# Eight more halved steps in three of 25 blocks of a fused FFT and FFN kernel

## The chip, the cores and the metric

The kernel runs on one core of one Trainium2 chip. The metric is the device time of one execution in microseconds. A core has five engines, each with an instruction queue of its own that is worked off in order: PE (TensorE: matmuls; PEld is its weight load), DVE (VectorE), ACT (ScalarE), POOL (GpSimd, which here mainly issues transfers) and SP (SyncE, which issues the stores). They wait for each other through semaphores.

## The reference

```python
def _attn_ref(x) -> np.ndarray:          # x: 8 x 3008 x 256
    X = np.fft.fft(x, axis=1)
    X = np.fft.fft(X, axis=2)
    return X.real.astype(np.float32)

def _moe_ref(x, w_in, w_out):            # 24064 x 256, 256 x 2048, 2048 x 256
    h = np.maximum(x @ w_in, 0.0)
    return (h * h @ w_out).astype(np.float32)
```

The real part of a two-dimensional Fourier transform of each of 8 batches gives 24064 rows of 256. Each row goes through a matrix to 2048 values, a Relu, a square, and a matrix back to 256.

## The kernel before

The transform is done by matrix products with tables of sines and cosines, after the input has been folded along its symmetries. It is real, so row k and row S - k of the result have most of their work in common. If P is the part from the cosine sums (tile `zc`) times the folded first matrix (`gh[:, 0]`) and Q the part from the sine sums (`zs`, `gh[:, 1]`), then one row's value ahead of the Relu is P + Q, and its mirror row's is P - Q, but for a correction of one row of the sine part (weights `wv`, spread sine row `eb`).

**Blocks and steps.** The columns of `zc` and `zs` (one for each pair of rows) are cut into 25 blocks, `w` = 0 to 24, of 240, 512, 376, 376, 512, 448 and then mostly 512 columns. The "third", "fourth" and "seventh" block are `w` = 2, 3 and 6, and the "fifth" and "eighth" `w` = 4 and 7. A block has 8 steps, 0 to 7; a step makes 256 of the 2048 values for the block's columns. They go, squared, into the tile `h2`, first all plain columns, then all mirrored ones. Blocks of less than 384 columns ahead of a wider one make the wider one take its steps in twos (`ng` = 2: the second and the fifth block); the blocks that the change touches take them one by one.

**A plain step** (`pq`, `turn`, `square`): PE makes P + Q in four matmuls over the block's width (lines 801 and 802), ACT applies the Relu (L811), the result is squared by DVE (L816) or, for the steps in the second list of the plan, by ACT (L814). PE then adds -2Q in place by two matmuls with a third matrix (L807), which makes the mirrored values; ACT applies the Relu (L811) and DVE squares (L816).

**A halved step** (`half_q`, `half_p`, `row_sum`, `halves`): PE makes Q alone in two matmuls (L826), ACT copies -2Q to `sn` (L834), PE adds P in place in two matmuls (L840), ACT copies P + Q to `hd` (L842). The rest is done by DVE, for one or two steps together as the plan groups them: the corrections `eb` x `wv` ("rows", L850, one for each 128 values), added to `sn` (L854), `hd` + `sn` into the mirrored half (L864), the Relu over both halves (L865) and the square into `h2` (L866). A halved step thus has four matmuls in place of six, and more work for DVE. L850 and L854 of a group are queued when its last step's Q is made; L864, L865 and L866 of a group are queued one step later, between the rows of the next group if that step is halved too.

**Between the two halves of a step** run, in this order, the step's list `at[s]` (folding of later batches, making of tables), a share of the second matrix product of the block before (`ffn2`, L680: 16 matmuls in most steps, 8 in some where that block is narrower; L695 copies out and SP stores), and a share of the sums `z` that make the next block's `zc` and `zs` (matmuls L536; ACT copies the plain part, L541 and L545; DVE makes the mirrored part, L552, when the last matmul of a sum is queued). The next block's first matmul (L801) reads `zc`.

**Work of single blocks.** In the third block a second pair of tables is made: arguments on DVE (L254 to L274), sine and cosine on ACT (L277, L280), then weights on DVE in the last step (L285). The z sums of the fourth block read them. The fold of batches on DVE there is L447 and L458, after which POOL copies edges into `spn` (L464 to L466), which some z matmuls read. `row_weights` (L632, L633) makes `wv`, with 16 small matmuls into one of the accumulators of the second product. POOL issues the spreading of a sine row for the next block (`row_spread`, L642, `eb`) near the end of a block, after step 5 or 6 in most, if the next block has halved steps.

**Buffers.** `sn` rotates over two tiles, `hd` over two buffers that it shares with the argument tile of the tables, `eb` over two that it shares with a table input, first-product accumulators (`ph`) over two, second-product accumulators over two, and `h1` over five.

**The plan.** For each block it lists the groups of halved steps and the plain steps that ACT squares. Before, the first three blocks have no halved step; the fourth has steps 1, 2 and 4; the fifth 2 and 3; the seventh 1, 2, 4 and 5, with ACT squaring in steps 0, 3 and 6.

```python
    PLAN = {
        6: (((1, 2), (3, 4), (5, 6)), (0, 7)),
        5: (((1, 2), (3, 4), (5,)), (0, 6, 7)),
        4: (((1, 2), (4, 5)), (0, 3, 6)),
        3: (((1, 2), (4,)), (0, 5, 6)),
        2: (((2, 3),), ()),
    }
```

Each engine's instructions run in the order in which the kernel's code queues them (`tc.manual_schedule()`); waits are put in from the tiles that are read and written.

Of the kernel before, what the change touches and what calls it, by code (L numbers as in the profile page):

```python
# [28 lines left out]
def kernel(  # L29
# [36 lines left out]
    }  # L66

    RQ = (1, 3, 5, 0, 2, 4)
# [14 lines left out]
    while g < TOT:  # L83
        n = min(FIRST[len(wins)] if len(wins) < len(FIRST) else WN, TOT - g)
# [4 lines left out]
    def win_of(col):  # L89
        return max(w for w in range(NW) if wins[w][0] <= col) if col < TOT else NW  # L90
# [491 lines left out]
    def run(*jobs):  # L582
        for j in jobs:
            j()
# [132 lines left out]
    def fold_jobs(i):  # L717
        f = folds[i] = fold_steps(i)
        return [f["d_even"], f["n_cos"], f["d_odd"], f["n_sin"], f["odds"], f["nyq"], f["even"], f["back"]]
# [11 lines left out]

    def plan(w):

        if w < 3:
            return (), ()
        if w < 5:
            return PLAN[3 if w == 3 else 2]
        first, late, main = w in first_at, w in late_at, w in fold_at
        n = 4 if main or late else 5 if first or w + 1 == NW or not need[w + 1] else 6
        return PLAN[n - (first and late)]  # L740

    def halved(w):

        return plan(w)[0]
# [4 lines left out]
    for w in range(NW):  # L749
# [5 lines left out]
        at = [[] for _ in range(NST)]  # L755
        post = [[] for _ in range(NST)]
        if w == 0:
            at[2] = [f0s["even"], f0s["back"]]
            at[0] = [lambda: run(*z0(0, 2)), lambda: run(*z0(1, 2))]
        elif w == 1:  # L760
            fj = fold_jobs(1)
            at = [fj[0:1], fj[1:3], fj[3:4], fj[4:5], [], [], [], []]
            post[5] = fj[5:6]
            lo, hi = 6, 7
        elif w == 2:
            te = table_steps()
            at = [[folds[1]["even"], lambda: te["freq"](), lambda: te["args"](0)], [lambda: te["turns"](0)], [lambda: te["mods"](0)],
                  [lambda: te["absm"](0)], [lambda: te["sins"](0)], [lambda: te["coss"](0)], [], [lambda: te["weigh"]()]]
            for st in range(4):
                at[st + 3] = at[st + 3] + f0s["late"][st : st + 1]  # L770
            at[7].append(folds[1]["back"])
        elif w in fold_at:
            fj = jobs_of.pop(fold_at[w])
            at = [fj[2:3], fj[3:4], fj[4:5], [], [], [], fj[6:7], fj[7:8]]
            post[6] = fj[5:6]
        elif w == win_of(col_of[1, 1]) - 1:
            for st in range(4):
                at[st] = folds[1]["late"][st : st + 1]
            lo = 4
# [6 lines left out]
            at[0] = at[0] + fj[0:1]  # L786
            at[1] = at[1] + fj[1:2]
        if w == 2:
            at[2].append(row_weights)
        zj, zl = [], []  # L790
        for u in need[w + 1]:
            zu = z_steps(u)
# [24 lines left out]

        two = {s: g for g in halved(w) for s in g}
        by_act = plan(w)[1]
        sns, hds = {}, {}  # L820

# [173 lines left out]
```

## Time and profile before

| what | value |
| --- | --- |
| median of 3 runs | 600.67 us (600.64 to 600.76) |
| the profiled execution | 600.49 us |
| its span, first to last instruction | 598.7 us |
| granted TensorE clock | full throughout |
| matmuls, weight loads | 4376 each |
| instructions of DVE, ACT, POOL | 747, 661, 152 |
| mean DMA rate over the span | 84 GB/s |
| PE's longest waits, by what ended them | DVE 3.8 (start), ACT sn L834 2.5 (nine), DVE 1.5 (start), DVE 1.2 (first block), DVE h L866 1.1 (two) |

The profile is of one execution. In its groups and timelines a row has a start and a duration in us (or a mean in ns), engine, line, operation, the tiles written and read, and a count; in square brackets stands the idle time ahead of it with what ended it. A row with "x4" is four instructions, its duration from the first start to the last end. A matmul's end is modelled: the next one is issued before it. On DVE and ACT too, an instruction that does not read the result of the one ahead starts a little before that one's shown end.

### The profile page before, as it was taken

How to read it: one execution, taken by the hardware profiler on the slowest of the kernel's cores; microseconds unless marked ns; L12 is line 12 of the kernel's file. 1: busy time of each engine (PE TensorE's matmuls, PEld its weight loads, DVE VectorE, ACT ScalarE, POOL GpSimd, SP SyncE). 2: the span in 40 equal slices, each digit the busy share in tenths (PEclk: the TensorE clock that was granted, in tenths of full speed). 3: DMA queues.
4: the chain of work that ended last, by engine and by line, in shares of the span. 5: the costliest groups of instructions: out<-in, count | busy, mean ns of one | idle time of the engine just before them, and what ended most of it. 6: DMA issues, size and time to landing. Idle time of an engine off the chain costs nothing.

```text
span 598.7 us, 11343 instructions
## 1 busy us (share of the span) xinstructions
PE 579.3 (97%) x4376; PEld 420.6 (70%) x4376; DVE 512.9 (86%) x747; ACT 514.0 (86%) x661; POOL 96.7 (16%) x152
## 2 busy tenths in 40 slices
PE   5899999999999999999999999999999999999996
PEld 2557776776777777777677776777777776776786
DVE  7897578886999987989889899898998799889980
ACT  7687788888999889989889898989989888888882
POOL 6350301202102023030112200412000120000000
PEclk9999999999999999999999999999999999999999
DMA  8945342472444635834355424555133361434122
GB/s 148 204 109 137 49 73 54 54 156 87 64 47 83 135 103 78 124 108 65 44 114 104 107 41 58 105 123 91 47 35 68 70 99 42 52 54 44 61 58 68
DMA packets 37581, 50.31 MB, mean 84 GB/s; under 512 B 4567, under 2 KB 30711, under 8 KB 37527
## 3 DMA queue, kind: packets, MB, share of 16 engines
q0 software_dynamic: 10400, 24.94, 32.0%
q1 hardware_dynamic: 26899, 24.44, 13.6%
q8 instruction: 34, 0.56, 0.4%
q10 hardware_dynamic: 228, 0.21, 0.1%
q14 instruction: 20, 0.16, 0.1%
HBM read 33.63 MB, written 27.84 MB: 103 GB/s over the span
## 4 chain that ended last, share of the span: by engine, by line
PE 67%; DVE 12%; ACT 12%; issue 7%; DMA 1%; POOL 0%; ACTq 0%; DVEq 0%; SPq 0%; POOLq 0%
PE po L680 40%; PE ph L840 5%; PE ph L807 5%; PE ph L801 5%; PE ph L802 5%; PE ph L826 5%; ACT h L811 3%; PE pz L536 3%; ACT sn L834 3%; ACT osb L695 2%; DVE h L866 2%; ACT hd L842 2%; DVE hd L865 2%; DVE hd L864 2%; DVE sn L854 1%
## 5 line engine op out<-in xcount | busy, mean ns | idle before, releaser
L680 PE MATMUL po<-wout,h 128*128 128x256 f16 (+1 forms) x3024 | 362.0, 273 | 1.1 <-DVE h L866 1.1
L680 PEld LDWEIGHTS <-h 128*128 128x128 f16 (+1 forms) x3024 | 296.5, 98 | 72.8 <-DVE h L866 1.7
L811 ACT ACTIVATE h<-ph 128x1024 f16<-128x1024 f32 (+3 forms) x196 | 185.6, 981 | 11.6 <-PE ph L807 8.6
L842 ACT ACTIVATE hd<-ph 128x1024 f16<-128x1024 f32 (+3 forms) x94 | 94.0, 1001 | 14.7 <-PE ph L840 13.3
L866 DVE TENSOR_TENSOR h<-hd 128x4096 f16<-128x4096 f16 (+6 forms) x51 | 105.3, 2065 | 1.4
L816 DVE TENSOR_TENSOR h<-h 128x1024 f16<-128x1024 f16 (+3 forms) x135 | 85.4, 656 | 24.7 <-ACT h L811 21.8
L834 ACT ACTIVATE sn<-ph 128x1024 f16<-128x1024 f32 (+3 forms) x94 | 93.6, 997 | 0.7 <-PE ph L826 0.7
L854 DVE TENSOR_TENSOR sn<-sn,hd 128x2048 f16<-128x2048 f16 (+6 forms) x51 | 56.7, 1113 | 22.6 <-ACT sn L834 18.0
L695 ACT ACTIVATE osb<-po 128x512 f32<-128x512 f32 (+3 forms) x95 | 54.6, 578 | 24.6 <-PE po L680 23.8
L801 PE MATMUL ph<-zc,gh 128*128 128x512 f16 (+3 forms) x196 | 72.1, 368 | 0.5 <-ACT h L897 0.3
L802 PE MATMUL ph<-zs,gh 128*128 128x512 f16 (+3 forms) x196 | 72.1, 368 | 0.0
L864 DVE TENSOR_TENSOR hd<-hd,sn 128x2048 f16<-128x2048 f16 (+6 forms) x51 | 56.6, 1110 | 14.0 <-ACT hd L842 12.1
L814 ACT ACTIVATE h<-h 128x1024 f16<-128x1024 f16 (+3 forms) x61 | 62.7, 1028 | 1.9
L865 DVE TENSOR_SCALAR hd<-hd 128x4096 f16<-128x4096 f16 (+6 forms) x51 | 56.8, 1113 | 1.5
L840 PE MATMUL ph<-zc,gh 128*128 128x512 f16 (+3 forms) x188 | 54.6, 372 | 3.5 <-ACT sn L834 2.5
L807 PE MATMUL ph<-zs,gh 128*128 128x512 f16 (+3 forms) x196 | 55.3, 368 | 0.2 <-ACT h L811 0.2
L826 PE MATMUL ph<-zs,gh 128*128 128x512 f16 (+3 forms) x188 | 54.5, 372 | 0.0
L850 DVE TENSOR_SCALAR hd<-eb,wv 128x512 f16<-128x512 f16 (+3 forms) x188 | 53.9, 345 | 0.4 <-DMA eb<-zs 0.4
L802 PEld LDWEIGHTS <-gh 128*128 128x128 f16 x196 | 19.1, 98 | 21.2 <-issue 1.0
L801 PEld LDWEIGHTS <-gh 128*128 128x128 f16 x196 | 19.1, 97 | 20.3
L826 PEld LDWEIGHTS <-gh 128*128 128x128 f16 x188 | 18.3, 97 | 20.9
L642 POOL DMA_DIRECT2D eb<-zs x22 | 13.2, 601 | 120.0 <-ACT zs L545 61.8
(145 smaller groups left out, 416.1 us busy)
## 6 DMA issues: line engine op xcount, KB each, us to landing
out_dram<-osb SPq DMA_DIRECT2D x77, 128.0 KB
xo<-in_x_dram POOLq DMA_DIRECT2D x7, 768.0 KB
scr<-ev POOLq DMA_DIRECT2D x8, 390.0 KB
eb<-zs POOLq DMA_DIRECT2D x19, 128.0 KB
rb<-scr POOLq DMA_DIRECT2D x16, 130.0 KB
out_dram<-osb SPq DMA_DIRECT2D x12, 94.0 KB
w<-in_moe_w_in_dram POOLq DMA_DIRECT2D x2, 512.0 KB
wout<-in_moe_w_out_dram POOLq DMA_DIRECT2D x1, 1024.0 KB
```

The costliest lines, as they stand in the source:

```text
L680: nc.tensor.matmul(po[0:m, j * D : (j + 1) * D], h2[:, fc, q : q + m], wout16[:, fc, :], start=(fc == 0 and (j == 0 or not four or i > 3)) ...
L801: nc.tensor.matmul(ph[:, a, 0:wn], gh[:, 0, f0 : f0 + P], zcw[:, 0:wn], start=True, stop=False)
L802: nc.tensor.matmul(ph[:, a, 0:wn], gh[:, 1, f0 : f0 + P], zsw[:, 0:wn], start=False, stop=True)
L807: nc.tensor.matmul(phs[s][:, a, 0:wn], gh[:, 2, f0 : f0 + P], zsw[:, 0:wn], start=False, stop=True, skip_group_check=True)
L811: nc.scalar.activation(h1[:, :, 0:wn], phs[s][:, :, 0:wn], AF.Relu)
L816: return [lambda: nc.vector.tensor_tensor(h2[:, 2 * s : 2 * s + 2, sg * wn : (sg + 1) * wn], hv, hv, op=ALU.mult)]
L826: nc.tensor.matmul(ph[:, a, 0:wn], gh[:, 1, f0 : f0 + P], zsw[:, 0:wn], start=True, stop=True)
L834: nc.scalar.activation(sns[g][:, i : i + 2, 0:wn], ph[:, :, 0:wn], AF.Copy, bias=0.0, scale=-2.0)
L840: nc.tensor.matmul(ph[:, a, 0:wn], gh[:, 0, f0 : f0 + P], zcw[:, 0:wn], start=False, stop=True, skip_group_check=True)
L842: nc.scalar.activation(hds[g][:, i : i + 2, 0:wn], ph[:, :, 0:wn], AF.Copy, bias=0.0, scale=1.0)
L865: lambda: nc.vector.tensor_scalar(out=hv, in0=hv, scalar1=0.0, scalar2=None, op0=ALU.max),
L866: lambda: nc.vector.tensor_tensor(h2[:, 2 * g[0] : 2 * g[-1] + 2, 0 : 2 * wn], hv, hv, op=ALU.mult),
```

## The change

Three blocks get another plan: the third gets the halved steps (2, 3) and (4, 5) with ACT squaring in the other four; the fourth (1, 2), (3, 4) and (5) with ACT squaring in 0, 6 and 7, in place of (1, 2) and (4) with 0, 5 and 6; the seventh (1, 2), (3, 4) and (5) with 0, 6 and 7, in place of (1, 2) and (4, 5) with 0, 3 and 6. As the third block now has halved steps, a sine row is spread for it at the end of the second. In the third block the sine of the tables moves from step 4 to step 3, the cosine from step 5 to step 4, and the row weights from step 2 to step 1.

```diff
         2: (((2, 3),), ()),
+        0: (((2, 3), (4, 5)), (0, 1, 6, 7)),
     }
...
-        if w < 3:
+        if w < 2:
             return (), ()
         if w < 5:
-            return PLAN[3 if w == 3 else 2]
+            return PLAN[(0, 5, 2)[w - 2]]
         first, late, main = w in first_at, w in late_at, w in fold_at
         n = 4 if main or late else 5 if first or w + 1 == NW or not need[w + 1] else 6
-        return PLAN[n - (first and late)]
+        return PLAN[n - (first and late) + (w == 6)]
...
-                  [lambda: te["absm"](0)], [lambda: te["sins"](0)], [lambda: te["coss"](0)], [], [lambda: te["weigh"]()]]
+                  [lambda: te["absm"](0), lambda: te["sins"](0)], [lambda: te["coss"](0)], [], [], [lambda: te["weigh"]()]]
...
         if w == 2:
-            at[2].append(row_weights)
+            at[1].append(row_weights)
```

## The prediction

> **What bounds the kernel now.** I read the busy times first, then the waits of TensorE, then the busy times by block, then the timelines of DVE, ACT and PE around the changed blocks. Blocks are counted from one and their steps from 0 to 7.
>
> ```profile
> PE 579.3 (97%) x4376; PEld 420.6 (70%) x4376; DVE 512.9 (86%) x747; ACT 514.0 (86%) x661; POOL 96.7 (16%) x152
> ```
>
> PE is busy nearly throughout, so a matmul taken away shortens the run if nothing else is late. The table by stretch (length, then PE, PEld, DVE, ACT, POOL) has the third to seventh block:
>
> ```profile
> 49.71:71.72 22.01, 22.01 (x194) 17.63 (x192) 15.82 (x35) 15.57 (x24) 3.04 (x8) 1.00 0.33 74
> 71.72:91.38 19.66, 18.98 (x161) 15.02 (x159) 13.60 (x28) 16.91 (x27) 2.85 (x3) 1.00 0.42 63
> 91.38:114.00 22.62, 21.74 (x163) 15.13 (x160) 20.10 (x32) 19.28 (x27) 2.86 (x5) 1.00 0.25 51
> ...
> 135.75:159.27 23.52, 23.07 (x166) 16.04 (x165) 18.84 (x30) 21.86 (x28) 4.77 (x8) 1.00 0.43 79
> ```
>
> DVE is idle for 6.2 us in the third block and 6.1 in the fourth, but for 2.5 in the fifth. The question is whether what DVE must deliver by a given time still arrives. Three deliveries matter. The DVE timeline of the fourth and fifth block:
>
> ```profile
> 71.67 0.60 DVE L285 TENSOR_SCALAR sin<-sin,wge 128x377 f16<-128x377 f16 x2
> ...
> 76.08 1.00 DVE L850 TENSOR_SCALAR hd<-eb,wv 128x376 f16<-128x376 f16 x4 [0.37 <-DMA eb<-zs]
> 78.23 0.94 DVE L854 TENSOR_TENSOR sn<-sn,hd 128x1504 f16<-128x1504 f16 x1 [1.15 <-ACT sn L834]
> 79.79 0.94 DVE L864 TENSOR_TENSOR hd<-hd,sn 128x1504 f16<-128x1504 f16 x1 [0.62 <-ACT hd L842]
> ...
> 95.44 0.69 DVE L447 TENSOR_TENSOR xt<-rb 128x1040 f16<-128x1040 f16 x1
> ...
> 103.50 0.42 DVE L458 TENSOR_TENSOR yt<-xt 128x520 f16<-128x520 f16 x1
> ```
>
> The weighted sine table (L285) is read by PE at 73.23 (z, L536). From 95.44 to 103.92 DVE has no gap, and its L458 ends in PE's wait in the fifth block:
>
> ```profile
> 105.17 0.34 PE L536 MATMUL pz<-cos,spn 128*128 128x94 f16 x2 [0.33 <-POOL spn L465]
> ```
>
> So lateness of DVE at 95.44 reaches PE. In the seventh block (DVE):
>
> ```profile
> 145.49 1.23 DVE L864 TENSOR_TENSOR hd<-hd,sn 128x2048 f16<-128x2048 f16 x1 [0.79 <-ACT hd L842]
> 146.75 1.23 DVE L865 TENSOR_SCALAR hd<-hd 128x4096 f16<-128x4096 f16 x1
> 148.01 2.29 DVE L866 TENSOR_TENSOR h<-hd 128x4096 f16<-128x4096 f16 x1
> 150.22 0.69 DVE L447 TENSOR_TENSOR xt<-rb 128x1040 f16<-128x1040 f16 x1
> ...
> 155.28 0.60 DVE L552 SCALAR_TENSOR_TENSOR zc<-es,pz 128x102 f16<-128x102 f32 x2
> 155.80 1.22 DVE L864 TENSOR_TENSOR hd<-hd,sn 128x2048 f16<-128x2048 f16 x1
> ```
>
> DVE has no gap from 145.49 on either. The eighth block's first matmul (L801, 159.27) reads this zc, which is ready 3.7 us ahead.
>
> **The change, part by part.** A halved step has four matmuls over the block's width in place of six. Issue spacing is 0.158 us at 376 columns (two L807: 71.40 to 71.72) and 0.216 at 512. Four, two and one more halved steps remove 8, 4 and 2 matmuls: 1.27 + 0.63 + 0.43 = 2.33 us of PE. ACT keeps two passes per step; the third block adds four squares of 0.83 (L814 at 73.61), 3.3 us. A halved pair at 376 columns costs DVE 1.00 (four L850) + 0.94 (L854) + 0.94 (L864) + 0.94 (L865) + 1.72 (L866) = 5.54, a plain square 0.55. Third block: two pairs, and 12 squares fewer (all 8 plain ones go to ACT or vanish, and 4 mirrored ones): 11.1 - 6.6 = +4.5. Fourth: one pair more, 4 squares fewer, +3.3. Seventh (rows at 182.18 to 185.98: 0.68 + 0.69 + 0.69 + 1.23, and two L850 of 0.29; two squares of 0.65 fewer): +2.6. Together 10.4 us of DVE.
>
> Starts below follow DVE's order in the changed program: the next start is 0.04 after the end when it reads that result (79.79 to 80.77), about 0.08 before the end when not.
>
> *Third block.* PE is not held: half products wait for ACT's sn, which I put 0.2 us or more ahead each time. The eb transfer that is new here can be issued at 48.7, is wanted at 58.2, and the longest one seen, 69.79 to 76.08, took 6.3: nothing, and if it were later than 59.6, a loss of the excess. On POOL it stands before scr<-ev, which DVE frees at 52.2, and holds nothing. Row weights a step earlier: 0.40 of PE (55.75 to 56.15) only changes places; step 2's FFN2 takes that accumulator, whose reader L633 ends at 54.5, before 55.84. The sine row (0.84) moves one step up among copies; around its present place ACT has no idle, so 0. The fourth block's first matmul moves from 71.72 to 70.49 and PE wants the table at 72.00.
>
> DVE: the square of step 1 waits for ACT (row weights push FFN2's end to 55.36, osb copy to 55.99, Relu until 56.68) and starts at 56.71. Then L271 57.17, rows 58.22; L854 waits for sn of step 3 (ACT: hd 58.10, sn 58.80 to 59.59) and starts at 59.62; L274 60.48, L447 60.94; L864 waits for hd of step 3 (sine, osb, hd: 61.55): 61.58, L865 62.56, L866 63.54, L447 65.18, rows 65.79, L854 66.83, L458 67.69, L864 68.03, L865 69.01, L866 69.99, L458 71.63, square 71.97, L285 from 72.43. The sine half that PE reads ends at 73.20. PE's 1.23 are gone: z starts at 73.24 as before at 73.23, and the turn at 73.44 against 73.63.
>
> *Fourth block.* POOL's queue has spn (after L458, 72.05) before the next eb issue, which so moves from 69.79 to 72.64. Landing is the unknown: 6.3 us by the same transfer before, with the same followers; below, any landing by 77.0, 4.4 after the issue, counts alike, for then L854 waits for sn of step 2 (78.0) and not for the rows. I take 6.3, as it is the same transfer: rows at 78.93 in place of 76.08. Then L854 79.97, L864 80.93, L865 81.91, L866 82.89, rows 84.53, L854 85.57, L552 zs 86.43, L864 86.95, a row, L865 88.06, a row, L866 89.17, L854 90.81, L552 zc 91.27, L864 91.80, L865, L866 92.96, two squares, then the fifth block's squares at 94.74 and 95.35, L447 at 95.96: 0.5 late. PE could start the fifth block at 90.46, waits for zc until 91.6 (before 91.38), and at L536 spn stands 0.5 later than before. With the early landing L854 starts at 78.04 and L864 at 79.58, 1.35 sooner, and the same chain gives 0.8 gained. So +0.5, bounds -0.8 and +0.5.
>
> *Seventh block.* Step 3 is now halved, so the pair (3,4) is finished in step 5 and stands in DVE's queue ahead of that step's zc. From 150.22: rows 150.83 (+0.61), L854 152.07, L447 153.21, L552 zs 153.82, L864 154.34, a row 155.48, L865 155.74, a row, L866 157.14, L854 159.34, L458 159.94, zc 160.28, its first part (0.25 of the 0.60) done at 160.53. PE, 0.5 ahead by then (the two matmuls, and a stall at 149.83 that ends up a little shorter), wants it at 158.8 and starts at 160.57 in place of 159.27: +1.3. It costs -0.5 if zc were in time. Behind it DVE reaches L390 at 164.92 in place of 162.67; the 0.90 idle before L864 at 169.55 takes back the excess over 1.3.
>
> Sum: 0.5 + 1.3 = 1.8 on the profiled execution's 600.49 (span 598.7, 1.8 around it) gives 602.3; it lies 0.18 below the median of the runs, 600.67, from which the same sum gives 602.5. I say 602.4.
>
> **Rivals.** (A) the above. (B) DVE keeps up and the matmuls decide: 600.5 - 2.3 = 598.2. It needs the sine half before 72.0, L447 before 94.5 and zc before 158.8, that is DVE 1.2 to 1.8 us quicker in each place than its rows; PE at 97% speaks for it, the gapless DVE rows from 145.49 against. (C) The fourth block's transfer lands early: -0.8 + 1.3, 601.0. In the trace eb took its long 6.3 while squares and L285 ran beside it; after the later issue DVE idles from 74 on. The Trainium skill, "SBUF — State Buffer", section "SBUF: two separate sides", has a mechanism for that: a DVE instruction in a two-port mode keeps GpSimd from writing descriptors of its own DMAs; by it the idle DVE would bring C's time. One landing with a wait is all the trace shows of it. (D) DVE's debt of the seventh block is not taken back and PE meets it again in the ninth: another 0.9, 603.2; the 0.90 idle speaks against. (E) DVE is what bounds these blocks, and all 10.4 us are paid: 610.9; the idle 6.2 and 6.1 speak against. The Trainium skill, "Perfetto Trace Analysis", section "Identifying the Most-Contended Engine", points this way, as it judges PE by weight loads (70% here) and DVE by its busy share (86%). That the change doesn't act is no case: the lists of halved steps are literal.
>
> **How the numbers follow.** A 0.60, B 0.10, C 0.20, D 0.08, E 0.02. Likeliest: A, 602.4, its own range 601.7 to 603.0. The range 600.7 to 603.4 leaves out B, E and part of D. 0.2% is 1.2 us, about what counts here as a change: slower (over 601.9) is D, E and A without 0.05: 0.65; within 0.2%: C, that 0.05 and 0.02 of B: 0.27; faster (under 599.5): 0.08.
>
> **What would show it.** An idle before the eighth block's first L801, released by DVE L552, of some 1.8 us: without it the seventh block's part is wrong. PE waiting for DVE L285 before L536 at 72 to 73.3. L850 of the fourth block waiting for the eb transfer until about 78.9, and L447 of the fifth at about 96. If 14 fewer matmuls come with no new idle before PE, B is right and my DVE order is not what binds.

## The result and the profile after

The changed kernel takes 601.74 us (median of 20 runs, 601.50 to 601.98), the kernel before 600.66 (20 runs beside them): a ratio of 1.0018, interval 1.0011 to 1.0024, or 1.08 us slower. (The title counts eight added steps; the plan adds seven: four, two and one.) In the changed kernel's profile every line number of the kernel is one higher than before, so L801 is L802 and L552 is L553; in runs whose edits add lines further up, the numbers behind those lines are higher again (L851 of the changed kernel is L852 in one of them). A ratio is worked out from all executions, a few of which take some 2 us longer in either kernel, and so differs below from the quotient of the medians by up to 0.0007.

The page's busy times of the changed kernel:

```profile
PE 576.4 (96%) x4362; PEld 418.7 (70%) x4362; DVE 522.2 (87%) x759; ACT 517.2 (86%) x665; POOL 101.1 (17%) x153
```

Fourteen matmuls are gone and PE is busy for 2.9 us less, while DVE has 9.3 us more to do. The time that PE saved and more than that went into waits. Three of TensorE's waits were not in the kernel before, or not at this size: for DVE's weighted sine table (L286), for POOL's `spn` (L466) and for DVE's `zc` (L553, twice). Where they lie is seen in PE's timeline of the changed kernel:

```profile
73.57 0.24 PE L537 MATMUL pz<-sin,xt 128*128 128x188 f16 x1 [1.14 <-DVE sin L286]
...
91.21 0.39 PE L802 MATMUL ph<-zc,gh 128*128 128x512 f16 x1 [0.25 <-DVE zc L553]
...
105.25 0.34 PE L537 MATMUL pz<-cos,spn 128*128 128x94 f16 x2 [0.97 <-POOL spn L466]
...
160.68 0.39 PE L802 MATMUL ph<-zc,gh 128*128 128x512 f16 x1 [1.64 <-DVE zc L553]
```

The table by stretch of the changed kernel (third, fourth, fifth and seventh block; length, then PE, PEld, DVE, ACT, POOL):

```profile
50.02:70.76 20.74, 20.74 (x187) 16.84 (x185) 17.59 (x34) 18.77 (x28) 1.01 (x3) 1.00 0.35 75
70.76:91.21 20.45, 18.50 (x156) 14.46 (x154) 16.43 (x32) 17.40 (x28) 4.75 (x8) 1.00 0.55 77
91.21:114.08 22.87, 21.61 (x160) 15.16 (x161) 22.50 (x37) 18.91 (x26) 2.85 (x5) 1.00 0.22 39
135.83:160.68 24.85, 22.81 (x164) 15.76 (x162) 20.25 (x32) 22.99 (x29) 5.12 (x8) 1.00 0.42 80
```

The profiled executions do not reach the third block at the same time: its first matmul stands at 49.71 before, at 50.02 here and between 49.65 and 50.38 in the runs below, and this spread does not follow the edits. So I measure blocks from that matmul. Before, the sixth block starts 64.29 us after it and the eighth 109.56; here 64.06 and 110.66. The third block is shorter by 1.27, the fourth longer by 0.79, the fifth by 0.25: together -0.23. The sixth is as long as before, the seventh is longer by 1.33 (24.85 against 23.52). The net is +1.10, next to +1.08 measured.

The DVE timeline of the changed kernel around the two places:

```profile
73.20 0.55 DVE L286 TENSOR_SCALAR sin<-sin,wge 128x377 f16<-128x377 f16 x2
...
78.39 1.00 DVE L851 TENSOR_SCALAR hd<-eb,wv 128x376 f16<-128x376 f16 x4 [2.72 <-DMA eb<-zs]
79.50 0.94 DVE L855 TENSOR_TENSOR sn<-sn,hd 128x1504 f16<-128x1504 f16 x1
...
90.86 0.61 DVE L553 SCALAR_TENSOR_TENSOR zc<-es,pz 128x135 f16<-128x135 f32 x2
...
95.53 0.70 DVE L448 TENSOR_TENSOR xt<-rb 128x1040 f16<-128x1040 f16 x1
...
154.43 1.22 DVE L865 TENSOR_TENSOR hd<-hd,sn 128x2048 f16<-128x2048 f16 x1
155.56 0.35 DVE L851 TENSOR_SCALAR hd<-eb,wv 128x512 f16<-128x512 f16 x1
155.83 1.22 DVE L866 TENSOR_SCALAR hd<-hd 128x4096 f16<-128x4096 f16 x1
156.96 0.35 DVE L851 TENSOR_SCALAR hd<-eb,wv 128x512 f16<-128x512 f16 x1
157.22 2.29 DVE L867 TENSOR_TENSOR h<-hd 128x4096 f16<-128x4096 f16 x1
159.42 0.69 DVE L855 TENSOR_TENSOR sn<-sn,hd 128x1024 f16<-128x1024 f16 x1
160.03 0.42 DVE L459 TENSOR_TENSOR yt<-xt 128x520 f16<-128x520 f16 x1
160.36 0.61 DVE L553 SCALAR_TENSOR_TENSOR zc<-es,pz 128x102 f16<-128x102 f32 x2
```

In the fourth block DVE stands idle for 2.72 us until the spread sine row has landed. In the seventh, `zc` for the eighth block stands behind L865, L866 and L867 of the group (3, 4) in a row without gaps, and PE starts the eighth block 0.32 us after zc's start.

### The profile page after: what moved, and what is told of

Same layout as the page of the kernel before. It is cut to its first block, busy times and chain, and to the rows that moved or that the text cites. A ratio compares the mean times of both kernels' runs of the same rounds, so it can differ in the third digit from the quotient of the medians.

```text
span 600.2 us, 11326 instructions
## 1 busy us (share of the span) xinstructions
PE 576.4 (96%) x4362; PEld 418.7 (70%) x4362; DVE 522.2 (87%) x759; ACT 517.2 (86%) x665; POOL 101.1 (17%) x153
## 4 chain that ended last, share of the span: by engine, by line
PE 62%; DVE 18%; ACT 10%; issue 7%; DMA 3%; POOL 0%; DVEq 0%; SPq 0%; ACTq 0%; POOLq 0%
PE po L681 36%; PE ph L841 5%; PE ph L827 5%; PE ph L808 4%; PE ph L802 4%; PE ph L803 4%; PE pz L537 3%; DVE h L867 3%; DVE hd L866 3%; DVE hd L865 3%; ACT h L812 2%; ACT sn L835 2%; DVE sn L855 2%; ACT hd L843 2%; DVE hd L851 2%
## 5 line engine op out<-in xcount | busy, mean ns | idle before, releaser
L812 ACT ACTIVATE h<-ph 128x1024 f16<-128x1024 f32 (+3 forms) x182 | 174.7, 993 | 8.6 <-PE ph L808 4.5
L843 ACT ACTIVATE hd<-ph 128x1024 f16<-128x1024 f32 (+3 forms) x101 | 99.8, 989 | 16.9 <-PE ph L841 15.4
L867 DVE TENSOR_TENSOR h<-hd 128x4096 f16<-128x4096 f16 (+6 forms) x55 | 111.8, 2032 | 1.5
L835 ACT ACTIVATE sn<-ph 128x1024 f16<-128x1024 f32 (+3 forms) x101 | 99.4, 986 | 0.6 <-PE ph L827 0.6
L817 DVE TENSOR_TENSOR h<-h 128x1024 f16<-128x1024 f16 (+3 forms) x117 | 75.1, 671 | 16.0 <-ACT h L812 15.5
L855 DVE TENSOR_TENSOR sn<-sn,hd 128x2048 f16<-128x2048 f16 (+6 forms) x55 | 60.3, 1096 | 21.9 <-ACT sn L835 18.8
L865 DVE TENSOR_TENSOR hd<-hd,sn 128x2048 f16<-128x2048 f16 (+6 forms) x55 | 60.2, 1094 | 12.7 <-ACT hd L843 11.5
L802 PE MATMUL ph<-zc,gh 128*128 128x512 f16 (+3 forms) x182 | 67.5, 371 | 2.2 <-DVE zc L553 1.9
L803 PE MATMUL ph<-zs,gh 128*128 128x512 f16 (+3 forms) x182 | 67.5, 371 | 0.0
L866 DVE TENSOR_SCALAR hd<-hd 128x4096 f16<-128x4096 f16 (+6 forms) x55 | 60.3, 1096 | 1.6
L851 DVE TENSOR_SCALAR hd<-eb,wv 128x512 f16<-128x512 f16 (+3 forms) x202 | 57.8, 345 | 2.7 <-DMA eb<-zs 2.7
L827 PE MATMUL ph<-zs,gh 128*128 128x512 f16 (+3 forms) x202 | 58.0, 369 | 0.0
L808 PE MATMUL ph<-zs,gh 128*128 128x512 f16 (+3 forms) x182 | 51.8, 371 | 0.1
L802 PEld LDWEIGHTS <-gh 128*128 128x128 f16 x182 | 17.7, 97 | 21.9 <-DVE zc L553 2.8
```

Of the source, the lines that this page charges most:

```text
L802: nc.tensor.matmul(ph[:, a, 0:wn], gh[:, 0, f0 : f0 + P], zcw[:, 0:wn], start=True, stop=False)
L803: nc.tensor.matmul(ph[:, a, 0:wn], gh[:, 1, f0 : f0 + P], zsw[:, 0:wn], start=False, stop=True)
L808: nc.tensor.matmul(phs[s][:, a, 0:wn], gh[:, 2, f0 : f0 + P], zsw[:, 0:wn], start=False, stop=True, skip_group_check=True)
L812: nc.scalar.activation(h1[:, :, 0:wn], phs[s][:, :, 0:wn], AF.Relu)
L827: nc.tensor.matmul(ph[:, a, 0:wn], gh[:, 1, f0 : f0 + P], zsw[:, 0:wn], start=True, stop=True)
L835: nc.scalar.activation(sns[g][:, i : i + 2, 0:wn], ph[:, :, 0:wn], AF.Copy, bias=0.0, scale=-2.0)
```

## The experiments

Each run was timed beside the kernel before, on the same chip; the medians of the kernel before were 600.57 to 600.68 us, so times of runs that were not timed side by side compare to about 0.1 us. Where a distance is given, it is from the third block's first matmul. Edits are against the changed kernel unless another is named.

**Seventh block alone** (against the kernel before):

```diff
-        return PLAN[n - (first and late)]
+        return PLAN[n - (first and late) + (w == 6)]
```

> Only the seventh block gets the new plan (five halved steps in place of four); the third and fourth blocks stay as before. Theory (DVE's late zc is the cost here, the other two blocks gave 0.2 us back): PE's first L801 of the eighth block starts about 1.3 us later than before, with an idle of 1.6 to 1.8 us ahead of it that DVE L552 ends, and the time is 1.3 us above before, 602.0 (ratio 1.0022). Rival 1 (the loss comes from the third and fourth block, the seventh only shows it later): no such idle and 0.4 to 0.5 us gained by the two matmuls that go, 600.2. Rival 2 (all of DVE's 2.6 us of added work is paid): 603.3.

602.05 us, ratio 1.0022 (1.0013 to 1.0031): 1.41 above before. The wait is there at its full size, in PE's timeline of this kernel:

```profile
161.13 0.39 PE L801 MATMUL ph<-zc,gh 128*128 128x512 f16 x1 [1.64 <-DVE zc L552]
```

The seventh block lasts 24.85, as in the changed kernel. This one halved step makes the whole loss and a little more.

**Third and fourth block alone:** the changed kernel without `+ (w == 6)`.

> Only the third and fourth blocks are changed; the seventh keeps its four halved steps. Theory: a gain of about 0.2 us, 600.4 (ratio 0.9997, not to be told from no change), with PE's wait of about 1.1 us for DVE's sine weights (L286) in the fourth block and of about 1.0 us for spn in the fifth as in the changed kernel. Rival (the transfer of eb lands as late as in the kernel before, 6.3 us after its issue, the recorded term): L851 waits until 78.9 and the time is 0.5 above before, 601.2. Rival (the savings of 12 matmuls are kept): 1.9 below, 598.8.

600.45 us, ratio 0.9994 (0.9985 to 1.0003); sixth block at 64.07, eighth at 109.34 against 109.56 before. Six halved steps are worth 0.2 us of the 1.9 that their matmuls took.

**Third block alone:**

```diff
-            return PLAN[(0, 5, 2)[w - 2]]
+            return PLAN[(0, 3, 2)[w - 2]]
...
-        return PLAN[n - (first and late) + (w == 6)]
+        return PLAN[n - (first and late)]
```

> Only the third block is changed (its four halved steps, the sine row spread for it, sine, cosine and row weights a step earlier); fourth and seventh as before. Theory: PE's wait for the sine table (1.1 us) eats the 1.27 us of the eight matmuls, eb lands 2 us later than before, but the fourth block with its three halved steps has 6 us of DVE idle to take that back: 600.4 to 600.6, no change that can be told. Rival (the third block keeps its 1.27, and the fourth loses a microsecond): 599.4. Rival (the later eb costs here already): 601.0 or more.

600.88 us, ratio 0.9999 (0.9990 to 1.0008); sixth block at 64.11. So up to there the third block gives 0.18 and the fourth's two more steps 0.05. The time as a whole does not show it: in this profiled execution PE waits 1.14 us for `h` at 548.1, in place of 0.79 in the other kernels, in a block that the edit leaves as it was. The late transfer is there, too, a wait of 2.69 before L851, but the fourth block with its three halved steps takes it back: PE's wait for spn stays at 0.32.

**Order of zc in the seventh block:**

```diff
-        lo, hi = 0, NST - 2 if w == 3 or w > 4 else NST - 1
+        lo, hi = 0, NST - 3 if w == 6 else NST - 2 if w == 3 or w > 4 else NST - 1
```

> The changed kernel, but the z sums in its seventh block are spread over steps 0 to 4 in place of 0 to 5, so that in DVE's queue zs comes ahead of the rows of the group (3, 4) and zc ahead of its L865. The same instructions, in another order. Theory (zc stands behind the group's 1.2 + 1.2 + 2.3 us of DVE work, and PE waits for it): the idle of 1.64 us ahead of the eighth block's first matmul goes, that matmul starts near 158.9 in place of 160.7, and the time is 1.4 to 1.8 us below the changed kernel's 601.7: 599.9 to 600.4, ratio to before 0.999. Rival 1 (DVE has 2.6 us more to do in this block and is full, whatever its order): the wait moves to the pair's h2 or to the ninth block, 601.4 to 601.8. Rival 2 (three steps in a row whose squares ACT takes, 6, 7 and 0, hold PE once DVE does not): a new wait of PE for ACT of about 1 us in steps 6 and 7, 601.0 to 601.4.

600.92 us, ratio 1.0009 (0.9999 to 1.0019): 0.8 below the changed kernel, half of what I expected. PE's timeline of this kernel shows where the rest went:

```profile
158.54 0.38 PE L802 MATMUL ph<-zc,gh 128*128 128x512 f16 x1
...
163.96 0.21 PE L537 MATMUL pz<-sin,yt 128*128 128x95 f16 x1
164.50 0.21 PE L537 MATMUL pz<-cos,spn 128*128 128x94 f16 x1 [0.33 <-POOL spn L466]
165.10 0.22 PE L537 MATMUL pz<-cos,spn 128*128 128x95 f16 x1 [0.39 <-POOL spn L467]
```

The eighth block starts at 108.78, 1.88 sooner than in the changed kernel, so the order of the queue was the cause and not the amount of work. But PE now comes to the spn copies ahead of them, which had been covered by the longer wait. From 163.96 to 165.10 PE issues two matmuls that took 0.08 in the kernel before (164.69 to some 164.77), and the ninth block starts only 0.82 sooner.

**The second fold a step earlier as well:** the edit above, and

```diff
+        if w == 6:
+            at[5], at[6] = at[5] + at[6], []
```

> As the kernel with the z sums of the seventh block over five steps (600.92), and in its seventh block the second fold L459 moves from step 6 to step 5, so that spn is ready earlier. Theory (0.72 us of what the early zc gave was lost again because PE waited 0.33 and 0.39 us in the eighth block for the two spn copies, which follow that L459): these two waits go and the time falls by 0.7 to 600.2. Rival (the rest was lost to ACT, which squares in steps 6, 7 and 0, or to DVE's added work): 600.9, no change, with the wait for another tile in the eighth or ninth block.

600.91 us, ratio 0.9997 (0.9988 to 1.0006): no lower than without it. The two waits did go, and the ninth block starts at 132.23 in place of 133.19. But in the tenth there is a wait that no kernel above has, in PE's timeline of this kernel:

```profile
209.11 0.49 PE L537 MATMUL pz<-sin,od 128*128 128x376 f16 x2 [0.50 <-DVE od L419]
```

By the end of the profiled span 0.19 of the 0.96 are left. Neither theory had this place; the rival had the kind of it, DVE's added work met again further on.

**The transfer of eb earlier:**

```diff
+            at[6].insert(0, lambda: row_spread(3))
...
-            if s0 == hi - 1 and ng == 1 and w + 1 < NW and halved(w + 1):
+            if s0 == hi - 1 and ng == 1 and w != 2 and w + 1 < NW and halved(w + 1):
```

> The changed kernel, but the transfer of eb for the fourth block is issued early in step 6 of the third block, ahead of the spn copies in POOL's queue (about 67 in place of 73.04). The same instructions, in another order. Theory (the 2.72 us that L851 waits for eb at 78.4 is what makes DVE late in the fourth block): rows run from about 76, L855 waits for ACT's sn until 78, the first L865 goes from 80.5 to about 79.9, DVE is 0.6 us sooner in the fifth block, PE's wait for spn there (0.97) shrinks by as much, and the time is 0.6 below the changed kernel's, 601.1. Rival (the wait is cover for something else that ends there, or DVE in the fifth block is bound later): 601.7, no change. Rival (the transfer just takes longer when issued while DVE works, the landing stays at 76 to 78): a gain of 0.2 or less.

601.32 us, ratio 1.0007 (0.9998 to 1.0017): 0.42 below the changed kernel; sixth block at 63.58, 0.48 sooner. DVE's timeline of this kernel:

```profile
75.94 0.99 DVE L852 TENSOR_SCALAR hd<-eb,wv 128x376 f16<-128x376 f16 x4
78.85 0.94 DVE L856 TENSOR_TENSOR sn<-sn,hd 128x1504 f16<-128x1504 f16 x1 [1.92 <-ACT sn L836]
80.41 0.94 DVE L866 TENSOR_TENSOR hd<-hd,sn 128x1504 f16<-128x1504 f16 x1 [0.62 <-ACT hd L844]
```

POOL issued the transfer at 59.27 already, not near 67, and the rows no longer wait. Of the 2.72 us, only 0.5 were on the path: the waits for ACT's sn (1.92) and hd (0.62), which the late rows had covered, now take the rest. PE's wait for spn fell from 0.97 to 0.39.

**The weights of the tables behind the fold, sine first, on top of that:**

```diff
-            for t in (cos_t, sin_t):
+            for t in (sin_t, cos_t):
...
-                  [lambda: te["absm"](0), lambda: te["sins"](0)], [lambda: te["coss"](0)], [], [], [lambda: te["weigh"]()]]
+                  [lambda: te["absm"](0), lambda: te["sins"](0)], [lambda: te["coss"](0)], [], [], []]
...
+            at[6].append(lambda: te["weigh"]())
```

> As the kernel with the early eb issue (601.32), and the table weights of the third block move from step 7 to the end of step 6, behind the fold L459, the sine half first. Theory (with eb out of the way, DVE in the fourth block waits 1.92 us for ACT's sn, which PE makes late because it waited 1.13 for the sine table): PE's wait falls to 0.2 to 0.4, and the time falls by 0.5 to 0.8, less what PE waits more for spn in the fifth block: 600.5 to 600.9. Rival (PE's wait for the sine table is hidden by DVE in the fifth block): 601.3, with a wait for spn of 1.1 in place of 0.39.

600.59 us, ratio 1.0000 (0.9991 to 1.0009): 0.73 less. PE's wait for the table fell from 1.13 to 0.22 for the sine and 0.21 for the cosine, and the wait for spn stayed at 0.41, so the gain was kept. With the transfer out of the way, PE's wait for the sine table is on the path.

**The weights earlier still, alone:** in the changed kernel, to step 5, ahead of both folds.

```diff
-                  [lambda: te["absm"](0), lambda: te["sins"](0)], [lambda: te["coss"](0)], [], [], [lambda: te["weigh"]()]]
+                  [lambda: te["absm"](0), lambda: te["sins"](0)], [lambda: te["coss"](0)], [lambda: te["weigh"]()], [], []]
```

> The changed kernel, but the weights of the tables (four DVE instructions, some 1.07 us) move from step 7 of the third block to step 5, ahead of the fold in DVE's queue. The same instructions, in another order. Theory (PE's wait of 1.14 us for the sine table in the fourth block is not what binds; DVE's late eb and rows are): the wait for sine goes, but everything between steps 5 and 7 comes 1.07 later on DVE, spn and with it POOL's eb issue too, so eb lands near 79.4 in place of 78.35, the first L855 goes from 79.5 to 80.6, PE waits some 2 us for spn in the fifth block in place of 0.97, and the time is about 1.0 above the changed kernel's 601.7: 602.7. Rival (PE's wait for the sine table is paid in full): 600.6. Rival (both count, in different places): 601.7, no change.

603.71 us, ratio 1.0046 (1.0032 to 1.0060): 2.0 above the changed kernel, where I had expected 1.0. PE no longer waits for the sine table, and the kernel is the slowest of all. DVE's timeline of this kernel in the fourth block, and PE's in the fifth:

```profile
79.91 1.00 DVE L851 TENSOR_SCALAR hd<-eb,wv 128x376 f16<-128x376 f16 x4 [5.21 <-DMA eb<-zs]
```

```profile
92.73 0.39 PE L802 MATMUL ph<-zc,gh 128*128 128x512 f16 x1 [2.16 <-DVE zc L553]
...
106.78 0.34 PE L537 MATMUL pz<-cos,spn 128*128 128x94 f16 x2 [0.97 <-POOL spn L466]
```

The chain is the one I named (fold later, spn later, POOL's issue later at 74.14 against 73.04, eb later, all of DVE later), but eb took 5.8 us from its issue in place of 5.3, and PE met the lateness in the fourth block (a wait of 0.89 for ACT's Relu, L812, at 87.39) and at zc, while its wait for spn stayed at 0.97. The sixth block starts at 65.65, 1.59 behind the changed kernel. The two profiled executions differ by about as much, 1.49 (603.44 and 601.95); the medians differ by 2.0, and the five executions of this kernel spread from 603.21 to 604.16.

**All reorderings:** early eb, weights behind the fold, zc over five steps, second fold of the seventh block earlier.

> All the reorderings together on the changed kernel: early eb issue, table weights behind the fold in step 6 with the sine half first, z sums of the seventh block over five steps, second fold of the seventh block a step earlier. Theory (each repair is worth what it is worth alone, as they lie in different blocks): 601.7 - 0.4 - 0.6 - 0.8 - 0.7 = 599.2, faster than the kernel before by 1.4 (ratio 0.9976). Rival (the blocks are coupled through DVE, which has 10 us more to do): 600.0 to 600.6. If every one of the fourteen matmuls' 2.33 us were kept: 598.3.

599.63 us, ratio 0.9982 (0.9973 to 0.9991). The repairs of the two places add up as far as the ninth block (131.10, against 132.23 with those of the seventh block alone and 132.90 before), and the tenth takes part of it. DVE's and PE's timelines of this kernel there:

```profile
204.60 2.29 DVE L871 TENSOR_TENSOR h<-hd 128x4096 f16<-128x4096 f16 x1
206.81 0.96 DVE L423 TENSOR_TENSOR ev<-ab 128x1560 f16<-128x1560 f16 x1
207.69 0.18 DVE L419 CAST od<-py 128x6 f16<-128x6 f32 x1
```

```profile
207.93 0.49 PE L537 MATMUL pz<-sin,od 128*128 128x376 f16 x2 [0.69 <-DVE od L419]
```

A copy of 0.18 that PE wants stands behind 0.96 of work whose result POOL sends out and DVE folds only from 221.1 on: the pattern of the seventh block once more.

**That copy ahead of ev in the ninth block, too:**

```diff
-            post[6] = fj[5:6]
+            if w == 8:
+                at[6] = fj[5:6] + at[6]
+            else:
+                post[6] = fj[5:6]
```

> As the kernel with all the reorderings (599.63), and in the ninth block DVE's small copy into od (L419, 0.18) is queued ahead of the 0.96 of ev in place of behind it. Theory (DVE's added work, once the waits of the third to eighth block are gone, meets PE in the tenth block, where PE waited 0.69 us for that copy): the wait at 207.9 goes and the time falls by 0.7 to 598.9. Rival (the debt of DVE is met again at the next thing PE needs from it): 599.4 to 599.6, with a new wait for DVE after 208.

598.68 us, ratio 0.9975 (0.9963 to 0.9987). The wait is gone and none took its place. The medians differ by 0.95 and the length of the tenth block by 0.87, where 0.69 of idle was shown.

**And the second fold of the fifth block a step earlier:**

```diff
-        if w == 6:
-            at[5], at[6] = at[5] + at[6], []
+        if w in (4, 6):
+            v = w - 2 + w // 6
+            at[v], at[v + 1] = at[v] + at[v + 1], []
```

> As the kernel before it in this list, and in the fifth block the second fold L459 moves a step earlier, to stand right behind the first, so that spn is ready some 2.4 us sooner on DVE. Theory: PE's wait of 0.39 for spn at 104.0 goes and the time falls by another 0.4, to 598.5, nearly the 598.3 at which all fourteen matmuls' savings are kept. Rival (the later wait takes it): 598.9, no change.

598.11 us, ratio 0.9959 (0.9946 to 0.9973): 2.5 us faster than the kernel before. The page's busy times of this kernel:

```profile
PE 577.0 (97%) x4362; PEld 418.8 (70%) x4362; DVE 522.0 (88%) x759; ACT 517.1 (87%) x665; POOL 95.4 (16%) x153
```

It has the same instructions as the changed kernel, the same DVE work to 0.2 us, and takes 3.6 us less.

**The same order without the halved steps:** the kernel before with all these reorderings.

> The kernel before, without any of the added halved steps, with the reorderings of the fastest version alone (eb early, weights behind the fold with the sine half first, z sums of the seventh block over five steps, both second folds a step earlier, od's copy ahead of ev). Theory (the reorderings only remove waits that the added DVE work made; the kernel before has but 0.33 us of them, for spn): 600.3, so that 2.2 of the fastest version's 2.46 us come from the halved steps. Rival (the order was worth it by itself, and the added halved steps give little): 599.0 or less. Rival (in the old plan the new order hurts, as ACT's cosine is late for the earlier weights): 601 or more.

600.41 us, ratio 0.9990 (0.9981 to 0.9999). In the fifth block 0.59 is gained, in the seventh 0.30 lost (23.82 against 23.52). Between this kernel and the fastest lies only the change itself, the halved steps and the table and row-weight steps moved for them: 600.41 - 598.11 = 2.30 us, or 2.19 with each taken against the kernel before beside it. That is near the 2.33 worked out for fourteen matmuls, but not block by block. PE's timelines of the fastest kernel in the fourth block, and of this one in the seventh:

```profile
72.32 0.24 PE L537 MATMUL pz<-sin,xt 128*128 128x188 f16 x1 [0.21 <-DVE sin L286]
72.77 0.24 PE L537 MATMUL pz<-cos,xt 128*128 128x188 f16 x1 [0.21 <-DVE cos L286]
```

```profile
149.71 0.59 PE L848 MATMUL ph<-zc,gh 128*128 128x512 f16 x2 [0.66 <-ACT sn L842]
```

From this kernel to the fastest the third block is shorter by 1.27, as worked out. The fourth is shorter by 0.16 and not by 0.63, as PE still waits there for both tables. The seventh is shorter by 0.84 and not by 0.43: in the old plan the new order lengthens PE's wait for ACT's sn to 0.66 (0.45 before), and in the fastest it is 0.24. The eighth is 0.10 longer: together 2.17. So that the sum comes so near to 2.33 is in part luck.

## Why the prediction was right, and where a term was off

The time on record was 602.4, with 601.7 to 603.0 as the likeliest case's own range; 601.74 stands at the lower end of it. By the division of chances there it falls among the times within 0.2% of before, which were given 0.27, and not among those over 601.9, which were given 0.65. The mechanism held, and one term of the sum was off. Step by step:

- *PE's saving.* 2.33 us of matmuls: the third block is shorter by exactly the 1.27 worked out. The rest is not seen by itself in any run, and the 2.30 by which the fastest kernel is ahead of its order alone is made up otherwise (0.16 in the fourth block, 0.84 in the seventh).
- *DVE's added work.* 10.4 us worked out, 9.3 by the pages of the profiles. The gap of 0.04 before an instruction that reads the result ahead holds from L864 on to L866; between L850 and L854, and between L854 and L864, it is 0.10 in the traces of both kernels.
- *Third block.* PE was not held (20.74 busy of 20.74). The start that the fourth block was given, 70.49, was 70.45 after taking off the 0.31 by which this execution was late; PE's z start, 73.24, was 73.26. The 1.23 of earlier arrival turned into a wait of 1.14 for the sine table, as said.
- *Fourth block: the term that was mis-sized.* I took 6.3 us for the transfer of eb, the one landing that the trace of before showed, and put the rows at 78.93 and the loss up to the fifth block at +0.5, with -0.8 for a landing at 77.0 or sooner. POOL's issue came at 72.73 (72.64 forecast; these times again less 0.31), but the landing took 5.3, the rows stood at 78.08, zc at 90.55 (91.27) and L448 at 95.22 (95.96). All of the chain behind it is 0.7 to 0.85 us earlier than written down, and the three blocks gave -0.23 in place of +0.5. The mechanism held: L851 waited for eb, and in the run with the early issue all that follows on DVE came sooner. The value lay between the two bounds, not at the one I chose. Rival C, the early landing with 601.0, was wrong by as much on its side.
- *Seventh block.* zc forecast at 160.28 and measured at 160.36, the eighth block's first matmul at 160.57 and 160.68, the price +1.3 and 1.33. The run of the seventh block alone shows that this term makes the whole loss, and the run with zc ahead of the group that it is the place in the queue.
- *The excess is taken back.* The eighth block lasts 23.35 (23.34 before), as forecast. That holds for the changed kernel only because PE itself was late. Rival D's debt, which I gave 0.08, is real: in the runs where zc came in time, PE met it at the spn copies in the eighth block and at od in the tenth. I had looked at the 0.90 of idle in DVE's queue and not at what PE takes from DVE before it.
- *Rivals B and E.* B's 598.2 was not to be had by the change as it stood. The same change in another order came to 598.11, but not as B has it: against the kernel before, 1.27 come from the third block, 0.16 from the fourth, 0.58 from the fifth, where no matmul was taken away and PE's wait for spn went, and 0.55 from the seventh, and the eighth loses 0.10. That DVE's 10 us would bind was wrong: the fastest kernel does the same work.

## What to carry to other kernels

When work is moved from a full engine to one with gaps, sum up neither engine; list what the full engine takes from the other, and look in the in-order queue at what stands ahead of each of these deliveries. The order in the queues of DVE and POOL was worth 3.6 us here with the amount of work unchanged. A small result that another engine waits for belongs ahead of large ones that are wanted later. After each repair look again at the waits further on: three times the removed wait had covered the next one.

## What the runs showed of the hardware that was not expected

The same transfer of one sine row to all partitions, for the same block, took 6.3 us from issue to use before (and in the run of the seventh block alone), 5.3 in the changed kernel (and in the four runs that leave its third block as it is), and 5.8 in the run with the earliest weights. So the time repeats with the order of the kernel. In these stretches DVE was busy for 3.19, 1.71 and 0.56 us. I had linked a shorter landing to an idle DVE, by the Trainium skill, "SBUF — State Buffer", section "SBUF: two separate sides", where a DVE instruction in a two-port mode holds the port that GpSimd writes its descriptors through. The three landings are not in the order of DVE's busy time, and the stretch with the least of it is not the shortest, so by that measure the rule does not account for them here; busy time is only a stand-in for what DVE's mode was. Nor do the rates of the DMA engines order them (97, 98 and 84 GB/s). What sets the landing stays open: no run varied it alone.

The idle shown ahead of a matmul is less than what the wait costs, since it is counted from the modelled end of the matmul ahead: 0.69 shown and 0.87 gained in the length of the block when it went (od), 0.39 shown and 0.65 gained in the same way (spn in the fifth block), and 0.72 shown in two waits where the starts of the matmuls give 1.06.
